# A recurrent attention with a gated MLP on one Trainium2 core: the attention's work written as a list of operations that the kernel sorts itself

## The chip, the cores and the metric

The kernel runs on one core of one Trainium2 chip. The time is the device's time for one launch in microseconds (us); three runs of the kernel before gave 843.01, 844.03 and 845.59, and their median, 844.03, is the number that the change is measured against. Five engines work side by side, each in its own fixed order of instructions: TensorE (PE in the profile; PEld is its loading of the stationary operand), VectorE (DVE), ScalarE (ACT), GpSimd (POOL) and SyncE (SP). They meet at semaphores. Here SP and POOL do little else than start transfers (DMA).

## The reference

A recurrence over 768 time steps for 4 x 8 heads of width 40, followed by an MLP over the 3072 tokens:

```python
state = np.zeros((B, H, D, D))                       # B, H, S, D = 4, 8, 768, 40
for t in range(S):
    y[:, :, t] = np.einsum('bhd,bhde->bhe', rt, state)
    Sa = np.einsum('bhde,bhe->bhd', state, at)
    state = state * wt[:, :, None, :] - np.einsum('bhd,bhe->bhde', Sa, bt)
    state = state + np.einsum('bhd,bhe->bhde', vt, kt)
x = y.transpose(0, 2, 1, 3).reshape(B * S, H * D)    # 3072 x 320
h = x @ w_in                                         # w_in 320 x 2048
g = h * np.tanh(np.log1p(np.exp(h)))
out = g @ w_out                                      # w_out 2048 x 320
```

The weights of the MLP come as 64-bit floats, everything else as 32-bit floats.

## The kernel before

**Attention in chunks.** The 768 steps are cut into 12 chunks of 64 (`C = 64`, `nch = 12`). Inside a chunk the recurrence becomes matrix products; only the state `ST` is carried from one chunk to the next. The 32 heads lie as two `be`, two `al` (on the partitions) and eight more, which a step takes in two halves `g`. The work has three parts:

- *Preparation*, `pre_a(c, be)`, 24 times. It loads the decays and `a` into `wa` and the rows of `b` and `k` into `bk` (L131 to L134, two buffers of each). On DVE it forms the running products of the decay, `P` forward (L147) and `E` backward (L157, written into `wa` over `a`, so that it stands behind the copies of `a` to `ad` by ACT, L155), and scales `a` (L152) and `bk` (L170). `P` goes to DRAM (L172, POOL's queue), for the MLP. PE multiplies `bk` by `ad` (L186); ACT and DVE take the results to `GP` and, masked, to `HA` (L188 to L193); PE transposes `bk` (L202), ACT copies it to `bkn`, and `bk` is free again.
- *Inverse*, `pre_inv(n)` and `post_inv(n)`, for two chunks at a time, six in all. DVE turns `GP` into `X` (`XL`, L209), does 30 pairs of a product (L214) and a sum (L216), in each of which every instruction needs the one before, and turns the result into `TT` (L218) and `T1` (L220). Then PE (L232, L241) and ACT make from it the blocks `bdT` (L249 to L251), and PE the operand `KT` of the recurrence from `HA` and `bdT` (L258, copied by ACT, L260).
- *Step*, `step(c)`, 12 times, each needing the step before. For each `g`: PE multiplies `KT` by `VS`, which holds the state and the values (L284), ACT takes it to `UVT` (L286), PE forms `pq` (L314) and transposes (L293, L304), DVE masks (L316), and PE sums output and new state (L334, L339); ACT copies the output to `yev` (L343), POOL's queue stores it (L370), and DVE updates the state (`stn` L342, `ST` L346).

**The MLP.** `M.run` takes 12 blocks of 256 tokens. `load_x` loads the attention's stored output and `P` and multiplies them (L565); `mlp1` (L583) is the first product with the weights split into a high and a low part, `mlp2` (L603 to L605) the second. Before it the weights are converted from 64 bits: a conversion loads a piece to `cv_d`, ACT writes a scaled copy to `cv_m` (L459), DVE puts the 32-bit number together in three instructions (L461 to L463) and ACT and DVE split it (L494, L495). `M.early` does the first quarter of `w_in`, `M.first` the other three, `M.second` three of the eight pieces of `w_out`, and `M.third`, within the MLP, the last five.

**What sets the order.** The order on each engine is made by the framework's scheduler, which takes instructions in the order of the program, as dependencies and free buffers allow, and moves parts of it ahead or back by an offset: `at(tc, k)` looks up the part's name in the table `OFF`, whose numbers are written by hand. `ORDER` says how steps, inverses and preparations follow each other in the program (the preparation of pair `n + 2` stands after the inverse of pair `n + 1`), `SORD` how the pieces of a step do. PSUM, eight banks, is cut into four pools of two: `ps_u` and `ps_q` for the steps, `ps_a` for the inverses, `ps_g` for the preparations; the MLP's matmuls use `ps_h` where `ps_a` and `ps_g` were.

Of the kernel before, what the change touches and what calls it, by code (L numbers as in the profile page):

```python
# [78 lines left out]
def attention(ctx, tc, I, yD, pD, nch, M):  # L79
# [35 lines left out]
    VS = [cs.tile([128, 2, 344], F32, name=f"VS{be}") for be in range(2)]
    UVT = cs.tile([128, 8, 256], F32, name="UVT")
    UVQ = [cs.tile([128, 16, 104], F32, name=f"UVQ{be}") for be in range(2)]
    bdr = [cs.tile([128, 2, 8, 2, 64], F32, name=f"bdr{i}") for i in range(NBR)] * (2 // NBR)
# [4 lines left out]
    RW, W2, HA, BKN, GP, KT = {}, {}, {}, {}, {}, {}
    LQ, SQ, OQ, PQ = (dict(S=SP, G=G, A=A)[x] for x in QS)

    def pre_a(c, be):
        n = 2 * c + be
        wa, bk, ad = wab[n % NWA], bkb[n % NWA], adb[n % 2]
        for al in range(2):
            q = slice(al * 64, al * 64 + 40)  # L130
            LQ.dma_start(out=wa[q], in_=I['wa'][c, be, al])  # L131
        for al in range(2):
            q = slice(al * 64, al * 64 + 40)
            LQ.dma_start(out=bk[q, :, 0:128], in_=I['bk'][c, be, al])  # L134
# [10 lines left out]
        V.tensor_reduce(out=w2[:, 0], in_=wz3[:, :, 1:33], axis=AX.X, op=ALU.mult)
# [512 lines left out]
```

## Time and profile before

| | before |
|---|---|
| runs | 843.01, 844.03, 845.59 us (median 844.03) |
| span of the profiled execution | 843.5 us |
| PE busy | 748.6 us (89%), 7816 instructions |
| DVE busy | 462.0 us (55%), 975 instructions |
| ACT busy | 429.0 us (51%), 937 instructions |
| POOL busy | 103.3 us (12%), 182 instructions |

The profile is of one execution, on its own clock from the span's start; its span is within the spread of the runs. In a row of instruction groups stand line, engine, operation, output and inputs with their shape, the count, then busy time and mean duration in ns, then the idle time of the engine just before them and what ended it. In a row of the timeline stand start, duration, engine, line, operation and shape, and in brackets how long it waited and for what. A weight load and its matmul are two records, and a row that joins several instructions gives their common stretch. L12 is line 12 of the kernel before, or, for lines of the changed kernel, of that one. Busy shares are means over stages with different limits, so a stage is read by itself.

### The profile page before, as it was taken

How to read it: one execution, taken by the hardware profiler on the slowest of the kernel's cores; microseconds unless marked ns; L12 is line 12 of the kernel's file. 1: busy time of each engine (PE TensorE's matmuls, PEld its weight loads, DVE VectorE, ACT ScalarE, POOL GpSimd, SP SyncE). 2: the span in 40 equal slices, each digit the busy share in tenths (PEclk: the TensorE clock that was granted, in tenths of full speed). 3: DMA queues.
4: the chain of work that ended last, by engine and by line, in shares of the span. 5: the costliest groups of instructions: out<-in, count | busy, mean ns of one | idle time of the engine just before them, and what ended most of it. 6: DMA issues, size and time to landing. Idle time of an engine off the chain costs nothing.

```text
span 843.5 us, 18796 instructions
## 1 busy us (share of the span) xinstructions
PE 748.6 (89%) x7816; PEld 695.6 (82%) x7816; DVE 462.0 (55%) x975; ACT 429.0 (51%) x937; POOL 103.3 (12%) x182
## 2 busy tenths in 40 slices
PE   2645898998989889889799899999999999999998
PEld 2534697887868778778768799999999999999998
DVE  6789879739899658788924639221222222122110
ACT  4533647774586866566738546333333333333331
POOL 8100012113122023221101200000000000000000
PEclk9855689899999999899959999999999999999999
DMA  6422223323423233323425734211120111100000
GB/s 177 134 71 64 74 63 73 90 67 105 129 81 80 66 88 103 82 67 96 123 66 142 179 109 128 54 35 36 38 54 25 31 54 35 35 21 16 16 1 32
DMA packets 58212, 61.91 MB, mean 73 GB/s; under 512 B 25536, under 2 KB 48704, under 8 KB 58128
## 3 DMA queue, kind: packets, MB, share of 16 engines
q1 hardware_dynamic: 49296, 40.94, 17.6%
q0 software_dynamic: 8832, 19.79, 9.5%
q8 instruction: 61, 1.00, 0.5%
q14 instruction: 23, 0.19, 0.1%
HBM read 48.79 MB, written 11.86 MB: 72 GB/s over the span
## 4 chain that ended last, share of the span: by engine, by line
PE 62%; DVE 15%; ACT 15%; issue 5%; DMA 2%; ACTq 0%; DVEq 0%; SPq 0%
PE ph L583 21%; PE po L604 7%; PE po L605 7%; PE po L603 7%; PE pa L186 5%; PE pa L258 4%; PE pq L314 3%; PE pq L334 2%; DVE XL L216 2%; DVE tmp L214 2%; ACT ad L155 2%; PE pu L284 1%; DMA cv_d<-in_wo 1%; DVE P L147 1%; ACT bdT L250 1%
## 5 line engine op out<-in xcount | busy, mean ns | idle before, releaser
L583 PE MATMUL ph<-xh,w_ih 128*128 128x256 f32 x576 | 148.3, 283 | 0.5 <-ACT xh L566 0.5
L585 ACT ACTIVATE g<-ph 128x512 f32<-128x512 f32 x96 | 57.3, 598 | 179.3 <-PE ph L583 179.2
L589 DVE TENSOR_TENSOR gl<-g,gh 128x1024 fp32r<-128x1024 f32 x48 | 58.7, 1225 | 160.7 <-ACT gh L588 160.4
L583 PE MATMUL ph<-xh,w_il 128*128 128x256 f32 x576 | 123.6, 283 | 0.0
L186 PE MATMUL pa<-bk,ad 128*128 128x168 f32 x384 | 85.0, 373 | 42.7 <-DVE bk L170 15.0
L604 PE MATMUL po<-w_ol,gh 128*128 128x320 f32 x384 | 118.8, 310 | 0.1
L605 PE MATMUL po<-w_oh,gl 128*128 128x320 f32 x384 | 118.4, 309 | 0.0
L603 PE MATMUL po<-w_oh,gh 128*128 128x320 f32 x384 | 117.7, 309 | 0.0
L186 PEld LDWEIGHTS pa<-bk,ad 128*128 128x128 f32 x384 | 70.8, 233 | 47.8 <-issue 22.8
L583 PEld LDWEIGHTS ph<-xh,w_ih 128*128 128x128 f32 x576 | 109.3, 190 | 0.7 <-ACT xh L566 0.7
L583 PE MATMUL ph<-xl,w_ih 128*128 128x256 f32 x384 | 101.2, 285 | 0.0
L583 PEld LDWEIGHTS ph<-xh,w_il 128*128 128x128 f32 x576 | 96.3, 190 | 0.0
L583 PEld LDWEIGHTS ph<-xl,w_ih 128*128 128x128 f32 x384 | 73.1, 190 | 0.8 <-issue 0.5
L604 PEld LDWEIGHTS po<-w_ol,gh 128*128 128x128 f32 x384 | 72.1, 188 | 0.5 <-DVE w_ol L495 0.5
L605 PEld LDWEIGHTS po<-w_oh,gl 128*128 128x128 f32 x384 | 72.1, 188 | 0.1
L603 PEld LDWEIGHTS po<-w_oh,gh 128*128 128x128 f32 x384 | 71.8, 188 | 0.0
L258 PE MATMUL pa<-bdT,HA 128*104 128x128 f32 x384 | 57.0, 304 | 9.0 <-ACT bdT L251 7.3
L258 PEld LDWEIGHTS pa<-bdT,HA 128*104 128x104 f32 x384 | 49.9, 190 | 14.4 <-ACT bdT L251 9.1
L216 DVE TENSOR_TENSOR XL<-XL,tmp 128x30 f32<-128x30 f32 (+9 forms) x180 | 59.0, 328 | 2.4
L214 DVE TENSOR_TENSOR tmp<-XL 128x30 f32<-128x30 f32 (+9 forms) x180 | 58.5, 325 | 2.5
L314 PE MATMUL pq<-bdr,UVT 128*128 128x128 f32 x384 | 57.3, 294 | 2.3 <-DVE UVQ L316 1.5
L314 PEld LDWEIGHTS pq<-bdr,UVT 128*128 128x128 f32 x384 | 50.8, 205 | 4.0 <-DVE UVQ L316 1.9
(89 smaller groups left out, 1243.5 us busy)
## 6 DMA issues: line engine op xcount, KB each, us to landing
wa<-in_wa SPq DMA_DIRECT2D x48, 162.5 KB
bk<-in_bk SPq DMA_DIRECT2D x48, 160.0 KB
cv_d<-in_wi SPq DMA_DIRECT2D x12, 512.0 KB
cv_d<-in_wo SPq DMA_DIRECT2D x8, 640.0 KB
pD<-P POOLq DMA_DIRECT2D x48, 81.2 KB, 2.2
VS<-in_vN POOLq DMA_DIRECT2D x24, 160.0 KB, 3.6
UVT<-in_vD POOLq DMA_DIRECT2D x24, 160.0 KB, 3.9
bdr<-in_rD POOLq DMA_DIRECT2D x24, 160.0 KB, 4.4
```

Of the source, the lines that this page charges most:

```text
L155: A.copy(ad[q, :, :, al], a[q].rearrange("p (s k t) -> p s k t", k=2, t=32))
L186: PE.matmul(pt[:, j], ad[:, s0 + j].rearrange("p k a t -> p (k a t)"), bk[:, s0 + j], start=(j == 0), stop=True, skip_group_check=True)
L214: V.tensor_tensor(out=tv, in0=X[:, i + 1:32, i:i + 1].broadcast_to([128, 31 - i, i]), in1=X[:, i:i + 1, 0:i].broadcast_to([128, 31 - i, i] ...
L216: V.tensor_tensor(out=X[:, i + 1:32, 0:i], in0=X[:, i + 1:32, 0:i], in1=tv, op=ALU.add)
L258: PE.matmul(pk[:, j], ha[:, s0 + j], bd[:, s0 + j].rearrange("p a t -> p (a t)"), start=(j == 0), stop=True, skip_group_check=True)
L314: PE.matmul(pq[:, s], UVT[:, g * 4 + s, be * 128:be * 128 + 128], br[:, be, g * 4 + s].rearrange("p a t -> p (a t)"), start=(s == 0), stop ...
L583: PE.matmul(o, w, x, start=(j == 0 and n == 0), stop=(n == 7), skip_group_check=True)
L585: A.activation(g[:, f0:f0 + 2], ph, AF.Mish)
L589: V.tensor_tensor(out=gl, in0=g, in1=gh.bitcast(F32), op=ALU.subtract)
L603: PE.matmul(po[k], gh[:, j, t], oh, start=(f == 0), stop=False, skip_group_check=True)
L604: PE.matmul(po[k], gh[:, j, t], ol, start=False, stop=False, skip_group_check=True)
L605: PE.matmul(po[k], gl[:, j, t], oh, start=False, stop=(f == 15), skip_group_check=True)
```

## The change

Every piece of the attention and of the early weight conversions becomes an operation of a list, `S.op(engine, cost, function, r=, w=)`: its engine, an assumed duration in us, what it reads and writes, and the function that issues its one instruction or its few of the same kind. From the reads and writes the list knows what each operation waits for. `Plan.order` then simulates the engines with the assumed durations: of the operations that can start within 0.05 us of the earliest it takes the one with the longest remaining path (`tail`), and puts the others off; the update of the state has 15 us added to its path (`LATE`). Sorted by the simulated starts, the operations are issued under `tc.manual_schedule()`, so that this order is the order on every engine, DMA issues included. The MLP's `run` is left to the scheduler as before, and is issued behind the list.

The instructions themselves stay, with these differences. PSUM is two pools of four banks, `psl` for the steps and `psr` for preparations and inverses, given out bank by bank. `E` has a tile of its own instead of lying in `wa`. `stn` has two buffers instead of one. A conversion scales `cv_d` in place, without `cv_m`; and the conversions are spread anew: the first quarter of `w_in` (`early`) as before from the start, quarters 1 and 2 (`first`, two buffers) once all preparations are issued, quarter 3 and three pieces of `w_out` (`second`, two buffers) once all preparations and inverses and the last step's operations stand. In the diff, cut to its core, the bodies of `pre_a`, `inv` and `step` are those of before with each call wrapped in `op`; two of them are shown.

```diff
-NA = 2
-NWA = 2
...
-OFF = {'I': 80, 'T1': 80, 'P00': -40, 'P10': 80, 'P11': 40, 'b0': 15, 'c0': 600, 'u0': -15, 'u1': 250, 'd0': 250,
...
-def at(tc, k):
-    return tc.high_priority(offset=OFF[k]) if OFF.get(k) else nullcontext()
+LATE = 15.0
...
+class Plan:
+    def __init__(self, look=0.05):
...
+    def order(self):
+        for o in reversed(self.ops):
+            o.tail = o.cost + o.lat + max((p.tail for p in o.post), default=0.0) + o.late
...
+            best = max((o for o in ready if o.eng == e and start[o] <= low[e] + self.look), key=lambda o: (o.tail, -o.i))
...
+        out.sort(key=lambda o: o.start)
+        return out
+    def issue(self):
+        bound = set()
+        for o in self.order():
+            for b in o.bufs:
+                if b not in bound:
+                    bound.add(b)
+                    b.t = b.pool[1][b.k]
+            o.fn()
...
-    ps_u = pool("ps_u", NU, space=PSUM)
-    ps_q = pool("ps_q", NQ, space=PSUM)
-    ps_a = pool("ps_a", NA, ictx, "right", space=PSUM)
+    ps_l = pool("ps_l", 1, space=PSUM)
+    ps_r = pool("ps_r", 1, ictx, "right", space=PSUM)
...
+    newL = S.pool("psl", 4, [ps_l.tile([128, 512], F32, name=f"pl{i}") for i in range(4)])
+    newR4 = S.pool("psr", 4, [ps_r.tile([128, 512], F32, name=f"pr{i}") for i in range(4)])
...
-        V.tensor_tensor_scan(out=E[:, 0:519][:, ::-1], data0=wz[:, 2:521][:, ::-1], data1=d1[:, 1:520][:, ::-1],
-                             initial=0.0, op0=ALU.mult, op1=ALU.add)
+        op('V', 1.15, lambda: V.tensor_tensor_scan(out=E[:, 0:519][:, ::-1], data0=wz[:, 2:521][:, ::-1], data1=d1[:, 1:520][:, ::-1],
+                                                   initial=0.0, op0=ALU.mult, op1=ALU.add), r=WZ + ['d1'], w=['E'])
...
+            op('V', 0.42, lambda: V.tensor_tensor(
+                out=st[:, :, 0:40].rearrange("p (s a) d -> p s a d", a=2), in0=stn.t.rearrange("p (s a) d -> p s a d", a=2),
+                in1=R.t.rearrange("p a s -> p s a").unsqueeze(3).broadcast_to([128, 4, 2, 40]), op=ALU.mult),
+               r=[(stn, 0), (stn, 2)] + [R], w=[('ST', g)], late=LATE)
...
+    M.early(S)
     for n in range(nds):
+        for c in (2 * n, 2 * n + 1):
+            for be in range(2):
+                pre_a(c, be)
+    preps = list(S.ops)
+    invs = []
+    for n in range(nds):
+        k = len(S.ops)
+        inv(n)
+        invs += S.ops[k:]
+        for c in (2 * n, 2 * n + 1):
+            step(c)
+    M.first(S, S.after(preps, lambda: (pctx.close(), M.open_first(S))))
+    M.second(S, S.after(preps + invs + S.ops[-1:], lambda: (ictx.close(), M.open_second(S))))
+    with tc.manual_schedule():
+        S.issue()
```

How the rows move is seen at three places. In such rows stand line, operation, output and inputs (a number behind a name tells buffers apart), shape, and how many alike follow each other. First DVE at the program's start, before: `wa_96` and `bk_98` belong to the first preparation, `cv_w` and `cv_d` to the first weight conversion.

```order
L461 TENSOR_SCALAR cv_w<-cv_m 128x512
L462 SCALAR_TENSOR_TENSOR cv_w<-cv_m,cv_w 128x512
L463 SCALAR_TENSOR_TENSOR cv_w<-cv_d,cv_w 128x512
L145 TENSOR_REDUCE w_138<-wa_96 128x8
L146 RECIPROCAL d_102<-w_138 128x8
L147 SCALAR_TENSOR_TENSOR P<-wa_96,d_102 128x520
L495 SCALAR_TENSOR_TENSOR w_il_928<-cv_w,w_ih_927 128x512
L150 COPY w_138<-P 128x8
L152 TENSOR_TENSOR wa_96<-wa_96,P 128x512
L156 RECIPROCAL d_102<-w_138 128x8
L157 SCALAR_TENSOR_TENSOR wa_96<-wa_96,d_102 128x519
L170 TENSOR_TENSOR bk_98<-bk_98,wa_96 128x8x128
```

And after, where the first preparation has `wa_88` and `bk_90`, the second `wa_89`:

```order
L264 TENSOR_REDUCE w_98<-wa_88 128x8
L264 TENSOR_REDUCE w_99<-wa_89 128x8
L265 RECIPROCAL d_94<-w_98 128x8
L266 SCALAR_TENSOR_TENSOR P_96<-wa_88,d_94 128x520
L268 COPY w_98<-P_96 128x8
L269 TENSOR_TENSOR wa_88<-wa_88,P_96 128x512
L270 RECIPROCAL d_94<-w_98 128x8
L271 SCALAR_TENSOR_TENSOR E<-wa_88,d_94 128x519
L265 RECIPROCAL d_94<-w_99 128x8
L277 TENSOR_TENSOR bk_90<-bk_90,E 128x8x128
```

The conversion's four instructions stood ahead of and among the first preparation's; now the first two preparations follow each other, and `E` is written to its own tile.

Second DVE in the middle of an inverse, before, the first one (L214 and L216 are its chain; L146 to L170 are preparations of later chunks):

```order
L214 TENSOR_TENSOR tmp<-XL 128x238
L146 RECIPROCAL d_102<-w_868 128x8
L216 TENSOR_TENSOR XL<-XL,tmp 128x17x14
L147 SCALAR_TENSOR_TENSOR P<-wa_97,d_102 128x520
L214 TENSOR_TENSOR tmp<-XL 128x240
L150 COPY w_868<-P 128x8
L152 TENSOR_TENSOR wa_97<-wa_97,P 128x512
L216 TENSOR_TENSOR XL<-XL,tmp 128x16x15
L170 TENSOR_TENSOR bk_98<-bk_98,wa_96 128x8x128
L214 TENSOR_TENSOR tmp<-XL 128x240
L156 RECIPROCAL d_102<-w_868 128x8
L216 TENSOR_TENSOR XL<-XL,tmp 128x15x16
```

And after, the second one (L343 and L346 are the chain, L472 the masks of a step):

```order
L346 TENSOR_TENSOR XL<-XL,tmp 128x20x11
L343 TENSOR_TENSOR tmp<-XL 128x228
L346 TENSOR_TENSOR XL<-XL,tmp 128x19x12
L343 TENSOR_TENSOR tmp<-XL 128x234
L346 TENSOR_TENSOR XL<-XL,tmp 128x18x13
L472 TENSOR_TENSOR UVQ_116<-pl_160,cst 128x8x64
L472 TENSOR_TENSOR UVQ_117<-pl_161,cst 128x8x64
L472 TENSOR_TENSOR UVQ_116<-pl_158,cst 128x8x64
L472 TENSOR_TENSOR UVQ_117<-pl_159,cst 128x8x64
L343 TENSOR_TENSOR tmp<-XL 128x238
L346 TENSOR_TENSOR XL<-XL,tmp 128x17x14
L343 TENSOR_TENSOR tmp<-XL 128x240
```

The chain's links stood among other chunks' preparation; now they follow each other, and in the middle stand the four masks of one step together.

Third PE behind an inverse of the middle of the attention, before (the fifth), with `TT` and `X` of the inverse (L232, L241, L258), a preparation's products and transposes (L186, L202), and a step (L284, from `KT` and `VS`):

```order
L232 MATMUL pa<-TT,GP 32x32
L186 MATMUL pa<-bk_99,ad_101 128x168 x6
L232 MATMUL pa<-TT,GP 32x32 x12
L186 MATMUL pa<-bk_99,ad_101 128x168 x2
L232 MATMUL pa<-TT,GP 32x32 x19
L202 MATMUL pa<-cst,bk_99 128x128 x8
L241 MATMUL pa<-X_4209,GP 32x32 x32
L258 MATMUL pa<-bdT_103,HA 104x128 x8
L284 MATMUL pu<-KT,VS_116 64x64 x8
L258 MATMUL pa<-bdT_104,HA 104x128 x8
L284 MATMUL pu<-KT,VS_117 64x64 x8
```

And after, behind the fourth inverse and the last products (L502) of the step that follows it; L306 and L329 are the preparation's products and transposes, L457 transposes the state:

```order
L502 MATMUL pl_159<-bdr,smd_142 64x2x64 x4
L306 MATMUL pr_165<-bk_90,ad_92 128x168 x2
L329 MATMUL pr_163<-cst,bk_90 128x128 x4
L329 MATMUL pr_164<-cst,bk_90 128x128 x4
L306 MATMUL pr_162<-bk_91,ad_93 128x168 x3
L457 MATMUL pl_160<-cst,ST_119 128x128 x4
L457 MATMUL pl_161<-cst,ST_120 128x128 x4
L306 MATMUL pr_165<-bk_91,ad_93 128x168 x3
L306 MATMUL pr_162<-bk_91,ad_93 128x168 x2
L329 MATMUL pr_163<-cst,bk_91 128x128 x4
L329 MATMUL pr_164<-cst,bk_91 128x128 x4
```

Preparation stood in between the inverse's and the step's matmuls; now the last of its products and its transposes, which free `bk_90` and then `bk_91`, stand behind the whole step.

More of the change, by code (lines that the diff above doesn't have):

```diff
@@ L110, in attention @@
         G.memset(b, 0.0)
-    for t in [d1] + [x.rearrange("p s k a t -> p (s k a t)") for x in adb[:NAD]]:
+    for t in [d1] + [x.rearrange("p s k a t -> p (s k a t)") for x in adb]:
         A.copy(t, z.broadcast_to(t.shape))
-    for t in bdT:
-        G.memset(t, 0.0)
[L115 to L118, printed above, removed]
@@ L119, in attention @@
-    ST = [cs.tile([128, 8, 64], F32, name=f"ST{g}") for g in range(2)]
-    for t in VS + [UVT] + bdr[:NBR] + ST:
-        G.memset(t, 0.0)
+    VS = tiles(cs, 2, [128, 2, 344], "VS")
+    UVT = cs.tile([128, 8, 256], F32, name="UVT")
+    UVQ = tiles(cs, 2, [128, 16, 104], "UVQ")
+    bdr = cs.tile([128, 2, 8, 2, 64], F32, name="bdr")
+    ST = tiles(cs, 2, [128, 8, 64], "ST")
+    newBKN = make(wk, NBKN, [128, 664], "bkn")
+    newKT = make(wk, NKT, [104, 8, 128], "KT")
+    newRW = make(wk, 4, [128, 2, 16], "rw")
@@ L300, in step_d, with tr @@
             return None
-        smd = wk.tile([128, 4, 128], F32, name="smd", bufs=2)
-        pt = ps_u.tile([128, 4, 128], F32, name="pu")
-        for s in range(4):
-            PE.transpose(pt[:, s], st[:, 2 * s:2 * s + 2].rearrange("p a d -> p (a d)"), ident)
-        A.copy(smd, pt)
+        smd, b = newSMD(), newL()
+        dv = lambda: view(b, full, 512, "p (s x) -> p s x", s=4)
+        def tr():
+            for s in range(4):
+                PE.transpose(dv()[:, s], st[:, 2 * s:2 * s + 2].rearrange("p a d -> p (a d)"), ident)
@@ new lines, in w_in, with w_out, cv @@
+    def w_in(self, wp, q):
+        self.ih.append(wp.tile([128, 3, 512], F32R, name=f"w_ih{q}"))
+        self.il.append(wp.tile([128, 3, 512], F32R, name=f"w_il{q}"))
+    def w_out(self, wp, q):
+        self.oh.append(wp.tile([128, 640], F32R, name=f"w_oh{q}"))
+        self.ol.append(wp.tile([128, 640], F32R, name=f"w_ol{q}"))
+    def cv(self, n, w, ctx=None):
+        p = self.tc.tile_pool(name=n, bufs=1, side="right")
+        p = ctx.enter_context(p) if ctx else self.cvx.enter_context(p)
+        return p.tile([128, w], F32, name="cv_w"), p.tile([128, w, 2], I32, name="cv_d")
@@ L533, in second, with first, open_second @@
+    def first(self, S, key):
+        new = S.pool("cva", 2)
+        ops = [self.plan_in(S, new, q, k, [key]) for q in (1, 2) for k in range(3)]
+        S.after(ops, lambda: self.cvx.close())
+    def open_second(self, S):
         self.ps_h = self.pool("ps_h", NH, space=PSUM)
-        if NQ1 < 4:
-            wp = self.wp = self.pool("w2b", 1)
-            with self.tc.tile_pool(name="cvb", bufs=CVB, side="right") as cv:
-                self.w_in(wp, cv, range(NQ1, 4))
         self.mpx = self.pool("mpx", 2)
@@ L539, in second @@
         self.mpa = self.pool("mpa", 2)
[L540 to L543 removed]
+        wp = self.pool("w2d", 1)
+        self.w_in(wp, 3)
+        for q in range(NO1):
+            self.w_out(wp, q)
+        self.cvx = ExitStack()
+        S.cvd[:] = [self.cv(f"cvd{i}", 640) for i in range(2)]
+    def second(self, S, key):
+        new = S.pool("cvd", 2)
+        ops = [self.plan_in(S, new, 3, k, [key]) for k in range(3)]
+        ops += [self.plan(S, new, lambda q=q: (self.oh[q], self.ol[q]), self.I['wo'][:, q * 640:(q + 1) * 640], [key], ('wo', q))
+               for q in range(NO1)]
+        S.after(ops, lambda: self.cvx.close())
```

607 lines of the change are left out of this document (348 added, 259 removed).

## The prediction

> **What bounds the kernel now.** After the page I cut the span into four stages by what ends each: the first inverse (99.2 us), the sixth and last inverse (418.2), the attention's last matmuls (494), the end. Columns: stretch, its length, then busy time (and instructions) of PE, PEld, DVE, ACT and POOL, granted TensorE clock, DMA share, GB/s.
>
> ```profile
> 0.00:99.20 99.20, 50.48 (x222) 42.35 (x222) 80.16 (x182) 44.58 (x121) 24.62 (x46) 0.74 0.38 106
> 99.20:418.20 319.00, 281.61 (x4062) 249.95 (x4062) 254.91 (x638) 214.18 (x545) 67.87 (x120) 0.95 0.34 88
> 418.20:494.00 75.80, 70.74 (x877) 58.56 (x878) 35.09 (x60) 41.61 (x85) 9.86 (x14) 0.86 0.46 115
> 494.00:843.50 349.50, 345.75 (x2663) 344.78 (x2659) 91.87 (x97) 128.68 (x187) 1.00 (x2) 1.00 0.15 42
> ```
>
> The last stage, the MLP, is TensorE without a gap, and the change does not touch it. The first is DVE (80 of 99 us) with PE half idle: no recurrence step can run before the first inverse. In the second no engine is full by itself: DVE 80%, PE 88%. Where the inverses stand, where the MLP ends and how fast it runs:
>
> ```profile
> L209 DVE STREAM_TRANSPOSE XL<-GP x6: 2090/2124/2155, 49.9 to 375.2; 128x1024 f32<-128x1024 f32 x6
> L218 DVE STREAM_TRANSPOSE TT<-XL x6: 1931/1976/2023, 97.2 to 416.2; 128x1024 f32<-128x1024 f32 x6
> L605 PE MATMUL po<-w_oh,gl x384: 307/308/414, 504.5 to 839.6; 128*128 128x320 f32 x192
> 550.00:750.00 200.00, 200.00 (x1525) 200.00 (x1525) 47.61 (x48) 70.92 (x102) 0.00 (x0) 1.00 0.14 38
> ```
>
> The first inverse begins at 49.9 (L209) and its result stands at 97.2 + 2.0 = 99.2: 49 us for one inverse. Six ends in 418.2 - 99.2 = 319 us make a period of 63.8 us for two chunks. The MLP has 48 calls of `mlp1` with 32 matmuls and 48 of `mlp2` with 24, 2688 in all; at 200 / 1525 = 0.131 us each it needs 352.5 us, and from the last matmul's end (839.9) to the span's end are 3.6 us. So my sum has four terms: first inverse T0, five periods P, the tail from the last inverse to the first MLP matmul, and 352.5 + 3.6.
>
> **Part 1, the first inverse.** Two groups hold the inverse's chain, and its links wait for each other:
>
> ```profile
> L216 DVE TENSOR_TENSOR XL<-XL,tmp 128x30 f32<-128x30 f32 (+9 forms) x180 | 59.0, 328 | 2.4
> L214 DVE TENSOR_TENSOR tmp<-XL 128x30 f32<-128x30 f32 (+9 forms) x180 | 58.5, 325 | 2.5
> ```
> ```profile
> 410.12 0.32 DVE L216 TENSOR_TENSOR XL<-XL,tmp 128x150 f32<-128x150 f32 x1
> 410.48 0.29 DVE L214 TENSOR_TENSOR tmp<-XL 128x130 f32<-128x130 f32 x1
> ```
>
> One inverse is (59.0 + 58.5) / 6 = 19.6 us of 60 links, 0.04 between links (410.12 + 0.32 to 410.48), say 2.1, and the transposes 2.1 and 2.0: 25.8 us when nothing stands between. The first one took 49, for the scheduler put other chunks' preparation between its links; in the new order two short masks stand there. Ahead of it are four preparations. They began late, with a conversion in front:
>
> ```profile
> 5.91 0.47 DVE L461 TENSOR_SCALAR cv_w<-cv_m 128x512 int32<-128x512 int32 x1 [2.84 <-ACT cv_m L459]
> ...
> 7.75 0.41 DVE L145 TENSOR_REDUCE w<-wa 128x8 f32<-128x256 f32 x1
> ```
> ```profile
> DVE wa L157 <- ACT ad L155: 11.0, 10, 2.9
> ```
>
> From 7.75 to 49.9 are 42.1 us. Out of it go three conversions of 7.75 - 5.91 and an L495 (512 wide, 0.7), 2.5 each, now behind the inverse, and three waits of L157 for ACT, 1.1 each (11.0 / 10), since `E` has a tile of its own: 31.3. They start at 5.9 instead of 7.75, so the inverse at 37.2. PE is as cold there as before (clock 0.74); for loads of `bk` that wait on it I allow 2. T0 = 39.2 + 25.8 = 65, against 99.2.
>
> **Part 2, the period.** Between two inverses the new order is a chain across engines. PE does post-inverse and one whole step first; only then the last preparation matmuls (L306) and the transposes (L329) that free a `bk` buffer; then the buffer is reloaded and multiplied (L277) on DVE, where the rest of two preparations and the inverse are queued behind. PE's and ACT's links at full clock:
>
> ```profile
> 372.59 0.84 PE L186 MATMUL pa<-bk,ad 128*128 128x168 f32 x4 [0.34 <-DVE HA L191]
> ...
> 382.72 1.99 PE L258 MATMUL pa<-bdT,HA 128*104 128x128 f32 x16
> ...
> 386.52 2.05 PE L314 MATMUL pq<-bdr,UVT 128*128 128x128 f32 x16 [0.33 <-ACT UVT L286]
> 388.41 1.04 PE L293 MATMUL pu<-cst,UVT 128*128 128x128 f32 x8
> ...
> 390.15 1.15 PE L284 MATMUL pu<-KT,VS 104*64 104x64 f32 x32
> ...
> 396.74 0.88 PE L334 MATMUL pq<-UVQ,bkn 128*64 128x104 f32 x16
> 397.45 0.61 PE L339 MATMUL pq<-bdr,smd 128*64 128x128 f32 x8
> ```
> ```profile
> 369.59 0.41 ACT L249 COPY bdT<-TT 32x256 f32<-32x256 f32 x1 [0.29 <-DVE TT L218]
> ...
> 377.83 1.49 ACT L251 COPY bdT<-pa 32x256 f32<-32x256 f32 x4
> ...
> 406.30 1.07 ACT L260 COPY KT<-pa 104x512 f32<-104x512 f32 x2
> ```
>
> (A matmul is two records, a transpose one; about 0.2 us at a row's end is overlapped by the next.) From TT's end: ACT makes eight bdT copies of 0.41, an X copy (512 wide, 0.54) and two short evictions (as one L249), to 4.2, then L251's four, to 5.7. PE's L393 waits for them: two rows like L258's, with PSUM handed back tile by tile, 4, to 9.7; hand-off 0.3 and the last KT copy, to 10.6. The step: L429's second row (as L284) to 11.8, with 0.3 and the UVT copy to 12.6; L469 (two rows like L314's, 3.5) starts on the first group at 12.1 and ends at 15.6; L442 (two like L293's, 1.8) to 17.4; four times L497 and L502 (0.72 + 0.44) to 22. Two L306 and eight L329 (as L293) make 1.5: the first `bk` buffer is free at 23.6. The second follows at 28, and its load is in before DVE comes to it. The reload, in a stretch with little else on the queues:
>
> ```profile
> 351.87 1.63 SPq L134 DMA_DIRECT2D bk<-in_bk  x2
> ```
> ```profile
> 355.00:356.00 1.00, 1.00 (x15) 0.88 (x16) 0.49 (x2) 0.00 (x0) 0.00 (x0) 0.79 0.39 113
> 356.00:357.00 1.00, 1.00 (x20) 0.93 (x16) 0.97 (x3) 0.42 (x1) 0.68 (x2) 1.00 0.00 0
> ```
>
> Issued at 351.9, nothing moves after 356: 4.1 to 4.3 us, so L277 starts at 27.9. DVE's prices:
>
> ```profile
> L316 DVE TENSOR_TENSOR UVQ<-pq,cst 128x512 f32<-128x512 f32 x48 | 32.9, 688 | 24.4 <-PE pq L314 24.3
> L147 DVE TENSOR_TENSOR_SCAN P<-wa,d 128x520 f32<-128x520 f32 x24 | 29.6, 1233 | 0.3
> L170 DVE TENSOR_TENSOR bk<-bk,wa 128x1024 f32<-128x1024 f32 x24 | 29.1, 1214 | 0.1
> L191 DVE TENSOR_TENSOR HA<-pa,cst 128x192 f32<-128x192 f32 (+1 forms) x72 | 23.7, 330 | 25.7 <-ACT HA L190 23.5 <-PE pa L186 2.0
> L346 DVE TENSOR_TENSOR ST<-stn,R 128x320 f32<-128x320 f32 x22 | 10.6, 484 | 0.1
> ```
>
> Independent instructions overlap by 0.08. From the first L277 to the inverse stand, in the new DVE order, two L277 (1.14 each), four scans (1.15), two L269 (as L316, 0.61), nine masks (L314 and L317, 0.27) and eight small ones (half a mask, an estimate): 2.3 + 4.6 + 1.2 + 2.4 + 1.1 = 11.6, with 0.4 for a mask that waits for its evictions 12. The inverse now carries the other step's DVE work and two masks between its links: four L472 (0.61), four L507 (as masks, 0.25), two L513 (0.4), 0.5, less 0.4 of hidden gaps: 25.8 + 4.3 = 30.1. P = 27.9 + 12 + 30.1 = 70. That other step's PE work (L393, then 11.4 us as above) runs under the inverse from 36 and ends, with the masks' wait, near 61; POOL's stores of P stand behind the step's yD, and are back before L277.
>
> Then the clock: PE rests some 9 us at the end of each inverse (61 to 70) and starts the chain cold:
>
> ```profile
> 352.18 3.58 PE L314 MATMUL pq<-bdr,UVT 128*128 128x128 f32 x16
> ```
> ```profile
> 348.00:355.00 7.00, 6.87 (x42) 5.73 (x41) 4.00 (x10) 2.19 (x5) 0.00 (x0) 0.54 0.11 32
> ```
>
> For 7 us the clock was half, and sixteen L314 took 3.58 instead of 2.05. One such spell at the start of a period costs between nothing (ACT's copies bind there) and 3.4; I take 2: P = 72, bounds 67 and 76. The Trainium skill, "TensorE: Matmul & The Clock Gate", section "HAM oscillation", has the rule that speaks against an order that lets PE rest: an idle window of about 3.4 us halves the clock, a busy one restores it. By that rule the spell lasts one window and P would be about 71.7 (an estimate); the trace agrees on the two levels, with a longer spell here.
>
> The last period has no later preparation on DVE, 2 less. T5, the last inverse's end, is 65 + 4 x 72 + 70 = 423, against 418.2: the start's 34 us are given back over five periods, which were 63.8 before since eight preparations ran ahead of the first.
>
> **Part 3, the tail.** What the new order has done by then is one step more and fewer conversions:
>
> ```profile
> 0.00:418.20 418.20, 8.69 (x18) 0.90 0.35 92
> ```
>
> (L346 alone: 18 of 22, so nine steps; three were left.) Now two are left, for one step stands behind each inverse and one inside it. Step 10 ends on PE 22 - 1.8 + 2 = 22 after the last inverse (no L306 between, the cold start), step 11 from the same links (VS copies 0.9, L429 2.2, UVT 0.9, L469 3.5, mask 1, L497 and L502 4.6) 13 later, 35. But of twelve conversions that DVE now does after the last inverse, ten stand ahead of the first MLP load's product, 17 of their instructions behind step 11's masks (at 33). At 0.47 (above) to 0.8, 0.65 each: 11, with ACT's turns 13, to 46. The product to the first MLP matmul took
>
> ```profile
> 465.67 0.96 DVE L565 TENSOR_TENSOR xy<-xy,xp 128x768 f32<-128x768 f32 x1 [0.66 <-DMA xp<-pD]
> ```
> ```profile
> 467.58 0.74 PE L583 MATMUL ph<-xh,w_ih 128*128 128x256 f32 x4 [0.47 <-ACT xh L566]
> ```
>
> 1.9, so the tail is 48 (bounds 37, PE alone, and 58). The last `w_in` quarter is converted under the first three; for its being late, 3.
>
> **The sum.** 423 + 48 + 3 + 352.5 + 3.6 = 830.1 against a span of 843.5. The runs' median, 844.0, is 0.5 above that span: 830.6.
>
> **Rivals.** (a) *Slower, by a cold PE.* From L393 to the free buffer PE's own links are 3.5 + 2.2 + 3.5 + 1.8 + 4.6 + 1.5 = 17.1 us at full clock. If the clock stays down through half of them more, each costs 0.75 more (3.58 / 2.05): 6.4 a period, 862. It decides from a mean P of 74.3 (65 + 5 x 74.3 + 407 = 843.5), 2.7 above mine: less than 4 us of such work. For it: the mean clock of 0.74 where PE was half idle; against it: 0.95 in the second stage, and the links stand close together. 21%. (b) *DVE hardly waits.* If PE and the reload come earlier than I add them, P falls to DVE's own work, 70 less the 9 that it now waits: 61, and the time to 776. For it: DVE's prices are the surest in the sum; against it: L277 waits for that buffer whatever else DVE does. 10%. (c) *The weights are late*,
>
> ```profile
> ACT cv_m L459 <- DMA cv_d<-in_wo: 5.1, 3, 2.8
> ```
>
> whose loads made ACT wait 1.7 in three cases. With 1.7 for each of the ten, the tail grows by 17: 848. For it: all loads are now behind the preparations; against it: two buffers instead of one. 7%. (d) *No change*: P of 74 gives the start's gain back exactly; 9%.
>
> **Numbers.** Forecast 53%, its own range 812 to 841 (P 68.5 to 74). The range 806 to 857 leaves out (b) and half of (a). Faster by over 0.3% (2.5 us, about what a measurement of this kernel can tell from no change): forecast and (b), 0.63; within, 0.09; slower, (a) and (c), 0.28.
>
> **What would show it.** TT's first end near 65, then ends 70 to 73 apart, the last near 423; DVE idle some 4 us ahead of an L277 and 5 more on the step's masks in each period; PE's clock at half under each inverse's end; the first MLP matmul near 471, none ahead of the attention's last. Wrong: a first TT beyond 75, periods under 66 or over 76, PE idle within the MLP.

## The result and the profile after

The changed kernel takes 892.44 us (median of four runs, 891.75 to 897.87) where the kernel before took 844.81 beside it: 5.85 per cent more, ratio 1.0585 with a 95% interval of 1.053 to 1.064. Run again later (e9), it took 894.64 beside 844.27, ratio 1.0605 (1.054 to 1.067). The profiled execution was the longest of the four, 897.87 us; that of e9 has a span of 890.7, so that differences of spans between runs are good to some 5 us. The forecast was faster: 830.6, in a range of 806 to 857. The kernel is slower instead, and the time lies above that range.

The stages of the profiled execution (span 895.7 us), cut at each inverse's end and at the first MLP matmul; columns as in the prediction.

```profile
0.00:72.40 72.40, 27.32 (x120) 23.50 (x120) 54.84 (x126) 24.47 (x66) 21.07 (x40) 0.70 0.39 97
72.40:154.56 82.16, 61.26 (x832) 57.36 (x832) 60.30 (x145) 46.82 (x122) 15.08 (x24) 0.81 0.30 80
154.56:237.09 82.53, 63.20 (x864) 58.88 (x864) 61.20 (x145) 47.50 (x123) 15.10 (x24) 0.83 0.31 80
237.09:318.15 81.06, 61.48 (x864) 56.63 (x864) 57.67 (x137) 45.64 (x120) 15.09 (x24) 0.86 0.28 75
318.15:400.05 81.90, 61.81 (x864) 57.15 (x864) 57.64 (x137) 45.72 (x120) 15.11 (x24) 0.85 0.28 74
400.05:481.26 81.21, 62.71 (x856) 58.46 (x856) 52.66 (x124) 44.26 (x117) 13.06 (x20) 0.84 0.23 63
481.26:536.66 55.40, 39.73 (x728) 38.12 (x728) 32.83 (x58) 35.99 (x75) 6.99 (x10) 0.78 0.51 158
536.66:895.70 359.04, 355.67 (x2688) 355.17 (x2688) 100.64 (x113) 135.13 (x195) 0.00 (x0) 0.99 0.16 44
```

The first inverse ends 26.8 us earlier than before (99.2 to 72.4). Then each period takes 81 to 82.5 us, almost alike, in which PE and DVE both rest for some 20 us: two engines with about 60 us of work each need 82, so for a good part of a period one of them works while the other waits. Over the five periods that is 408.9 us instead of 319, so the last inverse ends at 481.3, which is 63.1 later than the 418.2 of before. From there to the first MLP matmul pass 55.4 us instead of 49.4. The MLP's own stage is 16.9 shorter (359.0 against 843.5 - 467.6), since it no longer carries the attention's last steps. 63.1 + 6.0 - 16.9 is 52.2, the difference of the spans.

How a period passes: PE in the third one, TT standing at 237.09 (the timeline, rows that matter).

```profile
237.14 3.62 PE L361 MATMUL pr<-TT,GP 32*32 32x32 f32 x128 [8.14 <-DVE TT L348]
240.69 2.05 PE L306 MATMUL pr<-bk,ad 128*128 128x168 f32 x6
242.67 1.92 PE L369 MATMUL pr<-X,GP 32*32 32x32 f32 x64
244.52 2.05 PE L306 MATMUL pr<-bk,ad 128*128 128x168 f32 x6
246.36 4.42 PE L393 MATMUL pr<-bdT,HA 128*104 128x128 f32 x32
250.71 2.08 PE L429 MATMUL pl<-KT,VS 104*64 104x64 f32 x64
...
262.82 0.61 PE L502 MATMUL pl<-bdr,smd 128*64 128x128 f32 x8
263.36 0.84 PE L306 MATMUL pr<-bk,ad 128*128 128x168 f32 x4
264.03 1.04 PE L329 MATMUL pr<-cst,bk 128*128 128x128 f32 x8
```

Its continuation on SP's queue (the reload of the buffer that L329 freed) and on DVE:

```profile
265.33 1.60 SPq L249 DMA_DIRECT2D bk<-in_bk  x2
```
```profile
272.75 1.23 DVE L277 TENSOR_TENSOR bk<-bk,E 128x1024 f32<-128x1024 f32 x1 [5.44 <-DMA bk<-in_bk]
...
281.27 1.23 DVE L277 TENSOR_TENSOR bk<-bk,E 128x1024 f32<-128x1024 f32 x1 [1.55 <-DMA bk<-in_bk]
...
287.79 2.15 DVE L338 STREAM_TRANSPOSE XL<-GP 128x1024 f32<-128x1024 f32 x1
```

This is the closed chain of the prediction, link by link: inverse, PE's whole step, release of `bk`, reload, the rest of the preparation on DVE, inverse. Little of one link overlaps the next. An inverse takes DVE 26 to 32 us here, and from its end to the next one's start pass 50 to 52 (237.1 to 287.8 in this period). In the kernel before, with preparation between their links, the inverses took 37 to 50 us, and 3 to 43 passed between them, 18 on average.

### The profile page after: what moved, and what is told of

Its sections match the earlier page's. It is cut to its first block, busy times and chain, and to the rows that moved or that the text cites. A ratio compares the mean times of both kernels' runs of the same rounds, so it can differ in the third digit from the quotient of the medians.

```text
span 895.7 us, 18823 instructions
## 1 busy us (share of the span) xinstructions
PE 733.2 (82%) x7816; PEld 705.3 (79%) x7816; DVE 477.8 (53%) x975; ACT 425.5 (48%) x937; POOL 101.5 (11%) x166
## 4 chain that ended last, share of the span: by engine, by line
PE 66%; DVE 17%; DMA 6%; ACT 6%; issue 3%; POOL 1%; SPq 1%; DVEq 0%; ACTq 0%; POOLq 0%
PE ph L751 21%; PE pr L306 7%; PE po L772 6%; PE po L773 6%; PE po L771 6%; DVE XL L346 5%; DVE tmp L343 5%; DMA bk<-in_bk 4%; PE pl L469 3%; PE pr L393 3%; PE pl L497 3%; PE pl L442 3%; PE pr L361 2%; PE pr L369 2%; DMA wa<-in_wa 2%
## 5 line engine op out<-in xcount | busy, mean ns | idle before, releaser
L306 PE MATMUL pr<-bk,ad 128*128 128x168 f32 x384 | 97.3, 418 | 52.9 <-ACT HA L313 17.8
L306 PEld LDWEIGHTS pr<-bk,ad 128*128 128x128 f32 x384 | 82.2, 266 | 60.5 <-ACT HA L313 20.2
L751 PEld LDWEIGHTS ph<-xl,w_ih 128*128 128x128 f32 x384 | 73.8, 192 | 0.1
L361 PE MATMUL pr<-TT,GP 32*32 32x32 f32 x768 | 21.7, 236 | 61.7 <-DVE TT L348 53.2
L771 PEld LDWEIGHTS po<-w_oh,gh 128*128 128x128 f32 x384 | 72.2, 188 | 0.0
L773 PEld LDWEIGHTS po<-w_oh,gl 128*128 128x128 f32 x384 | 72.1, 188 | 0.0
L772 PEld LDWEIGHTS po<-w_ol,gh 128*128 128x128 f32 x384 | 72.1, 188 | 0.0
L361 PEld LDWEIGHTS pr<-TT,GP 32*32 32x32 f32 x768 | 21.0, 151 | 63.0 <-DVE TT L348 34.8
L346 DVE TENSOR_TENSOR XL<-XL,tmp 128x30 f32<-128x30 f32 (+9 forms) x180 | 59.6, 331 | 5.6
L343 DVE TENSOR_TENSOR tmp<-XL 128x30 f32<-128x30 f32 (+9 forms) x180 | 59.6, 331 | 5.5
L393 PE MATMUL pr<-bdT,HA 128*104 128x128 f32 x384 | 54.8, 309 | 2.7 <-ACT HA L313 1.0
L393 PEld LDWEIGHTS pr<-bdT,HA 128*104 128x104 f32 x384 | 52.8, 201 | 4.6 <-ACT KT L396 1.6
```

What stands on the lines that cost most here:

```text
L306: PE.matmul(pv()[:, j], ad[:, s0 + j].rearrange("p k a t -> p (k a t)"), bk[:, s0 + j], start=(j == 0), stop=True, skip_group_check=True)
L343: op('V', 0.16 + m * i * 0.001, lambda tv=tv, i=i, m=m: V.tensor_tensor(out=tv, in0=X[:, i + 1:32, i:i + 1].broadcast_to([128, m, i]), in1 ...
L346: op('V', 0.16 + m * i * 0.001, lambda tv=tv, i=i: V.tensor_tensor(out=X[:, i + 1:32, 0:i], in0=X[:, i + 1:32, 0:i], in1=tv, op=ALU.add), ...
L361: PE.matmul(xv()[al * 32:al * 32 + 32, j], gp.t[q, u, 0], TT[q, u], start=(j == 0), stop=True, skip_group_check=True)
L393: PE.matmul(kv()[:, j], ha.t[:, s0 + j], bd[:, o + s0 + j].rearrange("p a t -> p (a t)"), start=(j == 0), stop=True, skip_group_check=True)
L751: PE.matmul(o, w, x, start=(j == 0 and n == 0), stop=(n == 7), skip_group_check=True)
```

## The experiments

Theory A: the order makes a period one closed chain, because the whole step stands on PE between an inverse and the release of `bk`. Theory B: the half clock after PE's rest is what makes it long. Theory C: any fixed order costs this, since it can't react. The comparison of each run is with the kernel before, beside it on the chip. In the last column e5, e7, e10 and e12 have their first MLP matmuls ahead of the last step's last ones; the others follow from 518.1 in e5, 452.6 in e7, 551.9 in e10 and 491.4 in e12.

| run | us | before | ratio (95%) | inverses end | first MLP matmul |
|---|---|---|---|---|---|
| changed kernel | 892.44 | 844.81 | 1.0585 (1.053 to 1.064) | 72.4 to 481.3 | 536.7 |
| e1 LATE 10 | 851.03 | 839.87 | 1.0113 (1.006 to 1.017) | 73.8 to 432.0 | 487.9 |
| e2 no reload of bk | 874.35 | 839.87 | 1.0402 (1.034 to 1.046) | 68.1 to 460.8 | 514.5 |
| e3 no step loads | 892.48 | 839.87 | 1.0616 (1.056 to 1.068) | 72.3 to 475.0 | 530.4 |
| e4 PE kept busy, 32 | 890.40 | 839.87 | 1.0587 (1.052 to 1.066) | 72.2 to 474.9 | 529.3 |
| e5 conversions early | 882.05 | 842.95 | 1.0453 (1.039 to 1.052) | 72.1 to 478.8 | 510.3 |
| e6 third bk buffer | 874.26 | 842.95 | 1.0377 (1.031 to 1.045) | 74.6 to 457.6 | 512.9 |
| e7 other numbers | 812.73 | 842.95 | 0.9638 (0.957 to 0.971) | 83.1 to 407.3 | 443.6 |
| e8 other numbers, third buffer | 825.49 | 842.95 | 0.9789 (0.973 to 0.985) | 76.6 to 407.6 | 462.9 |
| e10 scheduler | 908.54 | 844.27 | 1.0772 (1.071 to 1.084) | 87.0 to 506.0 | 540.8 |
| e11 PE kept busy, 38 | 879.02 | 844.27 | 1.0418 (1.036 to 1.048) | 71.5 to 463.9 | 517.5 |
| e12 e7 with loads of 2.5 us | 851.72 | 844.27 | 1.0103 (1.007 to 1.014) | 76.6 to 443.6 | 479.8 |

**e1.** One number of the list:

```diff
-LATE = 15.0
+LATE = 10.0
```

> One number of the list, LATE, is 10 instead of 15: the same operations, but the transposes that free the bk buffers (L329) stand ahead of the step's matmuls on PE and not behind them. Theory A (a period is one closed chain, in which the whole step stands between an inverse and the reload of bk): the step's 12 to 15 us leave the chain, periods of 68 to 72 us instead of 82, 830 to 850 us in all. Theory B (PE's half clock after its rest makes the period long, whatever the order): the rest under the inverse stays, periods of 79 or more, 880 us or more. Theory C (any fixed order costs this, since it can't react to what the chip does): 870 to 895 us.

The period falls from 81.8 to (432.0 - 73.8) / 5 = 71.6 us, as theory A has it; the time, 851.03, is 1 us above A's range and far below those of B and C. The same instructions, sorted with one other number, are 4.5 per cent faster (1.0113 against 1.0585). The clock still falls in this kernel (0.53 from 226 to 237, behind an inverse), so B does not carry the 52 us. The one number moves other operations too, so e1 shows what the order is worth, and not the place of these transposes alone. Where the `bk` transposes now stand, PE's order behind the fourth inverse (L393 makes the step's KT):

```
L361 MATMUL pr_165<-TT,GP_153 32x32 x32
L369 MATMUL pr_165<-X_156,GP_153 32x32 x32
L306 MATMUL pr_165<-bk_91,ad_93 128x168 x3
L306 MATMUL pr_163<-bk_91,ad_93 128x168 x3
L306 MATMUL pr_162<-bk_91,ad_93 128x168 x2
L329 MATMUL pr_164<-cst,bk_91 128x128 x4
L329 MATMUL pr_165<-cst,bk_91 128x128 x4
L393 MATMUL pr_163<-bdT_102,HA_148 104x128 x4
```

The buffer is free before the step begins, and not behind it.

**e2.** The loads of `bk` only for the first chunk (L277's multiply is a minimum for the later ones):

```diff
-            op('S', 0.1, lambda q=q, al=al: SP.dma_start(out=bk[q, :, xo:xo + 128], in_=I['bk'][c, be, al]), w=[('bk', be, al)], lat=2.5)
+            op('S', 0.1, lambda q=q, al=al: SP.dma_start(out=bk[q, :, xo:xo + 128], in_=I['bk'][c, be, al]) if c == 0 else None, w=[('bk', be, al)], lat=2.5)
```

> bk is loaded for the first chunk only, later preparations work on what is in the buffers (their loads of bk and the use of that data are left out; the multiply of L277 becomes a minimum for them); the order on every engine is that of the changed kernel. Theory A: L277 follows PE's release of the buffer instead of a landing 7.4 us later, for the first of the two buffers in full and for the second in part: 7 to 9 us less in each of five periods, 848 to 860 us. Theory B: the clock is as before, a gain of at most the 5 us per period that DVE waited: 867 us or more.

15 to 18 us faster (by the ratios and by the medians), half of what I expected of A: 874.35 lies above A's range, and in the one that I had given to B. DVE in its third period, TT standing at 225.0:

```profile
256.17 1.22 DVE L277 TENSOR_TENSOR bk<-bk,E 128x1024 f32<-128x1024 f32 x1
259.83 0.42 DVE L264 TENSOR_REDUCE w<-wa 128x8 f32<-128x256 f32 x1 [2.44 <-DMA wa<-in_wa]
...
271.87 2.16 DVE L338 STREAM_TRANSPOSE XL<-GP 128x1024 f32<-128x1024 f32 x1
```

The L277 comes 31.2 us after TT instead of 35.7. Then DVE waits 2.44 for the next load, that of `wa`, where the changed kernel does not wait at this place; when the inverse begins, 3.8 of the 4.5 us are left (271.87 - 225.0 = 46.9 after TT instead of 50.7). The reload is a link, and not the largest.

**e3.** The step's loads left out after the first chunk, those of UVT and in the same way those of VS and bdr:

```diff
-            op('G', 0.75, lambda q=q, al=al: G.dma_start(out=UVT[q, :, 64:192], in_=I['vD'][c, al]), w=[('UVv', al, 0), ('UVv', al, 1)], lat=2.5)
+            op('G', 0.75, lambda q=q, al=al: G.dma_start(out=UVT[q, :, 64:192], in_=I['vD'][c, al]) if c == 0 else None, w=[('UVv', al, 0), ('UVv', al, 1)], lat=2.5)
```

> The loads of the step's VS, UVT and bdr are left out after the first chunk (the later chunks work on its data); the order is otherwise that of the changed kernel. Theory A with contention (the reload of bk takes 7.4 us instead of the 4.2 of my sum because the step's loads are issued in the same microseconds): landing 4.5 to 5.5 us after issue, 2 to 3 us less per period, 875 to 883 us. If the reload takes 7.4 us by itself: no change, 889 to 895 us.

No change in the time. The reload lands little earlier:

```profile
261.77 1.63 SPq L249 DMA_DIRECT2D bk<-in_bk  x2
```
```profile
268.04 1.23 DVE L277 TENSOR_TENSOR bk<-bk,E 128x1024 f32<-128x1024 f32 x1 [4.29 <-DMA bk<-in_bk]
```

268.04 - 261.77 is 6.3 us where the changed kernel has 7.4. The step's loads are worth 1 us of it, so contention with them falls as the main reason. Contention as such does not. The two loads of `bk` are 0.33 MB. In the changed kernel the DMA engines moved 1.33 MB from the issue to the L277 (178 GB/s for 7.45 us), here still 0.99 MB (158 GB/s for 6.27 us), for the stores of the step's output and the loads of `wa` go on beside them. In the quiet stretch of the prediction they moved 0.33 MB in 4.13 us, these loads alone. No run leaves the stores and `wa` out, so that their traffic is the reason is likely and not shown.

**e4 and e11.** Matmuls of the identity ahead of the first L361 of each inverse but the first, 32 in e4 and 38 in e11:

```diff
             def mx(h=h, xv=xv, b=bx):
+                for _ in range(32 if h == 0 and n else 0):
+                    PE.matmul(b.t[:, 0:128], ident, ident, start=True, stop=True, skip_group_check=True)
```

> 32 matmuls of the identity with itself (7.7 us at full clock) are put ahead of the first L361 of each inverse but the first, into the PSUM bank that L361 then overwrites: PE does not rest in the last 8.5 us of an inverse. Theory A: the granted clock under the inverse's end goes from 0.5 to near 1, but behind it ACT's copies bind, so 3 to 4 us less per period, 870 to 880 us. Theory B: the half clock is what makes the period long: 7 to 10 us less per period, 842 to 860 us.

> As e4, with 38 matmuls of the identity instead of 32 (8.7 us for a rest of 8.5), since in e4 a rest of 1.4 us was left and the clock fell again behind three of five inverses. Theory A: the clock holds behind all inverses, 3.4 us less per period as where it held in e4 (77.7 instead of 81.1), 872 to 880 us where the changed kernel has 889 to 892. Theory B: 850 us or less.

In e4 a rest of 1.0 to 1.4 us was left, and its time lies in neither theory's range. That rest made a difference. PE behind two inverses of e4, and the clock behind them (stretches as before, the clock is the third number from the right):

```profile
237.50 2.21 PE L363 MATMUL pr<-TT,GP 32*32 32x32 f32 x128 [1.02 <-DVE TT L348]
...
315.19 2.69 PE L363 MATMUL pr<-TT,GP 32*32 32x32 f32 x128 [1.43 <-DVE TT L348]
```
```profile
237.00:242.00 5.00, 4.50 (x199) 4.21 (x199) 5.00 (x6) 4.30 (x11) 0.00 (x0) 1.00 0.08 14
...
315.00:320.00 5.00, 4.81 (x142) 4.39 (x144) 5.00 (x8) 3.89 (x10) 0.00 (x0) 0.66 0.08 16
320.00:325.00 5.00, 5.00 (x77) 4.81 (x74) 3.75 (x10) 3.12 (x10) 1.02 (x2) 0.50 0.26 87
```

Behind the rest of 1.02 us the clock held, and that period took 77.7 us; behind the four of 1.43 to 1.44 it fell, and e4's mean period was 80.5, where e9 has 80.7. In e11, without a rest, it is 1.00 in the same places. There the first period, behind the inverse that has no such matmuls ahead of it, still takes 82.2; the four others take 77.5 on average, where e9 has 80.8 and the first profile 81.7. So a cold start costs a period 3.3 to 4.2 us. The time is 15.6 us below e9's beside it, as A had it (872 to 880). The clock is worth these 15.6 us, and the roughly 35 us that remain of the loss are not its doing: B falls as the whole reason and stands as a part.

**e5.** The six conversions of `first` ahead:

```diff
         ops = [self.plan_in(S, new, q, k, [key]) for q in (1, 2) for k in range(3)]
+        for o in ops:
+            o.late = 100.0
```

> The six conversions of first (quarters 1 and 2 of w_in) have 100 us added to their path in the list, so that they are taken as soon as they can start; nothing else is changed. Theory A for the tail (PE's 14.7 us of rest ahead of the MLP are the first load of x, which waits for the last of these six conversions): PE's rest ahead of the first MLP matmul falls to 1 to 5 us, 8 to 13 us less in all, 879 to 884 us. Rival: the conversions that come after them are late in their place, or the inverses wait for them: 888 to 896 us.

10.4 us faster by the medians, as expected. In the changed kernel PE rested 14.72 ahead of the MLP, and the load of x left SP's queue when the last of these conversions was done:

```profile
521.46 0.69 DVE L652 SCALAR_TENSOR_TENSOR w_il<-cv_w,w_ih 128x512 fp32r<-128x512 f32 x1 [0.70 <-ACT w_ih L651]
```
```profile
522.18 0.33 SPq L606 DMA_DIRECT2D xy<-yD  x1
```
```profile
536.66 1.23 PE L751 MATMUL ph<-xh,w_ih 128*128 128x256 f32 x4 [14.72 <-ACT xh L734]
```

In e5 that load is issued at 454.0. Two MLP matmuls stand at 510.3, ahead of the last step's, and the others follow from 518.10, right behind the attention's last (517.56 + 0.61). From the last inverse to there are 39.3 us, where the changed kernel has 55.4 (54.1 in e9).

**e6.** A third `bk` buffer, and the buffers taken in turn:

```diff
-    bkb = tiles(cp, 2, [128, 8, 168], "bk")
+    bkb = tiles(cp, 3, [128, 8, 168], "bk")
...
-        wa, bk, ad = wab[be], bkb[be], adb[be]
+        bi = (2 * c + be) % 3
+        wa, bk, ad = wab[be], bkb[bi], adb[be]
```

> A third bk buffer, taken in turn; costs and LATE as in the changed kernel, the list sorts itself anew. Theory A in the form that the buffer closes the chain: a preparation no longer waits for the release of a buffer by the matmuls behind the step, DVE's 7 us of waiting for bk per period go, periods of 72 to 76 us, 855 to 868 us. Theory A in the form that the step's place on PE closes it, whatever the buffers (the last products of a preparation stay behind the step): periods of 79 or more, 880 us or more.

874 us and periods of 76.6, between the two forms. The wait of DVE for `bk` shrinks from 31.9 to 23.4 us in total and does not go: the last products of a preparation still stand behind the step. DVE's masks of `HA` wait 25.4 us for these products, where the changed kernel has 8.3.

**e7, e8 and e12.** Other numbers of the list; e7's (the 5.1 stands for the other loads and for yD's store as well, and goes back to 2.5 in e12):

```diff
-LATE = 15.0
+LATE = 4.8
...
-    def __init__(self, look=0.05):
+    def __init__(self, look=0.08):
...
-            op('S', 0.1, lambda q=q, al=al: SP.dma_start(out=wa[q], in_=I['wa'][c, be, al]), w=[('wz', be, al), ('a', be, al)], lat=2.5)
+            op('S', 0.1, lambda q=q, al=al: SP.dma_start(out=wa[q], in_=I['wa'][c, be, al]), w=[('wz', be, al), ('a', be, al)], lat=5.1)
...
-            op('P', 0.29 * m, mm, r=[('ad', be, 0), ('ad', be, 1), ('id', be)] + BK, w=[b], mode=128, claim=[gp, ha])
+            op('P', 0.29 * m, mm, r=[('ad', be, 0), ('ad', be, 1), ('id', be)] + BK, w=[b], mode=128, claim=[gp, ha], late=2.0)
...
         ops = [self.plan_in(S, new, q, k, [key]) for q in (1, 2) for k in range(3)]
+        for o in ops:
+            o.late = 100.0
```

> The list with other numbers: LATE 4.8 instead of 15, a load assumed to take 5.1 us instead of 2.5, 2 us added to the path of the preparation's products (L306) and 100 to that of first's conversions, and a choice among operations that start within 0.08 us. Two bk buffers as before. Theory A: preparation no longer stands behind steps, and the load of x is not late: periods of 62 to 68 us, the last inverse near 400, 815 to 830 us. Theory C (a fixed order as such is dearer than the scheduler's): not below 840 us.

> The list with other numbers and a third bk buffer: LATE 11.3, a load assumed to take 3.9 us, 9.6 us added to the path of the transposes (L329), 2 to that of L306 and 10 to that of first's conversions, a choice within 0.02 us. Theory A: as e7, with the last inverse near 395, 813 to 828 us. Theory C: not below 840 us.

> As e7, but a load is again assumed to take 2.5 us. If the list's wrong duration for loads is a large part of the loss (loads land 4 to 7 us after their issue): preparation again waits for loads in its place and the order loses most of what e7 won, 850 to 885 us. If LATE and the two added paths make e7's order: 813 to 825 us.

e7 beats both kernels: 812.73 us, 3.6 per cent below the kernel before and 9 below the changed one, with the same instructions in a fixed order; that is 2 us below its range of 815 to 830. e8 is within its range. Both are well below the 840 of C, so a fixed order is not dear as such. DVE's rest ahead of the instructions that first use the loads of `bk` and `wa` (the groups of instructions; the last column), first in the changed kernel, then in e7, then in e12:

```profile
L277 DVE TENSOR_TENSOR bk<-bk,E 128x1024 f32<-128x1024 f32 x24 | 29.0, 1208 | 31.9 <-DMA bk<-in_bk 31.9
...
L264 DVE TENSOR_REDUCE w<-wa 128x8 f32<-128x256 f32 x24 | 9.7, 404 | 16.8 <-DMA wa<-in_wa 16.8
```
```profile
L277 DVE TENSOR_TENSOR bk<-bk,E 128x1024 f32<-128x1024 f32 x24 | 29.2, 1218 | 4.1 <-DMA bk<-in_bk 3.6
...
L264 DVE TENSOR_REDUCE w<-wa 128x8 f32<-128x256 f32 x24 | 9.6, 405 | 7.5 <-DMA wa<-in_wa 7.5
```
```profile
L277 DVE TENSOR_TENSOR bk<-bk,E 128x1024 f32<-128x1024 f32 x24 | 29.3, 1219 | 27.2 <-DMA bk<-in_bk 17.2 <-PE pl L429 5.1 <-PE pr L306 4.9
...
L264 DVE TENSOR_REDUCE w<-wa 128x8 f32<-128x256 f32 x24 | 9.8, 416 | 26.2 <-DMA wa<-in_wa 18.8 <-PE pr L289 7.4
```

That is 48.7 us in the changed kernel, 11.6 in e7 and 53.4 in e12, where only the assumed duration of a load went back to 2.5 us, and 39 us of e7's gain went with it. These waits alone do not make the time: e12 has more of them than the changed kernel and is 41 us faster. And e12 loses in one place. Its second period takes 113.2 us where e7's takes 73.1; its four others together take 253.9, e7's 251.1. In that period the third inverse takes DVE 75 us (182.0 to 257.3), with whole preparations between its links.

Such preparations stand between the links of e7's inverses too, as in the kernel before: from the second on an inverse takes 47 to 53 us there, and from its end to the next one's start pass 1 to 26. In the changed kernel these were 26 to 32 and 50 to 52. e7's first inverse ends later than the changed kernel's (83.1), and its periods of (407.3 - 83.1) / 5 = 64.8 us are those of the kernel before (63.8). PE goes to the first MLP matmuls, which stand inside the attention's last step, without a gap:

```profile
442.72 1.09 PE L457 MATMUL pl<-cst,ST 128*128 128x128 f32 x8
443.57 0.36 PE L753 MATMUL ph<-xh,w_ih 128*128 128x256 f32 x1
```

**e9** is the changed kernel again (above); its mean period is 80.7 us where the first profile has 81.8. **e10** issues the sorted list without `tc.manual_schedule()`:

> The changed kernel once more, beside the three that follow, as the measure for them: 5.3 to 6.4 per cent over the kernel before, as at its first run.

> The list is sorted and issued as in the changed kernel, but without the manual schedule: the framework's scheduler takes the operations in the list's order and moves them as it does in the kernel before. Theory A (it is this order that is bad, above all the step ahead of the last preparation): the scheduler brings preparation forward in part, periods of 70 to 78 us, 845 to 880 us. Theory C (a fixed order as such is the loss): within 1 per cent of the kernel before.

e10 is slower still, 908.54 us, with periods of 83.8, outside both expectations: C falls, and with it my expectation of A that the scheduler would mend the order. It starts from the list's order, puts conversions ahead of the first preparation again, and ends the first inverse at 87.0.

## Why the prediction was wrong, step by step

The sum had four terms against the span. Measured, they were: T0 72.4 instead of 65 (+7.4), five periods 408.9 instead of 358 (+50.9), the tail 55.4 instead of 48 (+7.4), and the MLP with its late weights 359.0 instead of 352.5 + 3.6 + 3 = 359.1. Together 65.6, the distance from 830.1 to 895.7. The step that failed is the period P of part 2, taken as 72 and measured as 81.8: its 50.9 us alone turn a gain of 13 us into a loss. The mechanism was right, a closed chain across the engines; the links that were off were all taken too short. P was already longer there than the 63.8 of before; what the sum counted on was the early first inverse, and a chain of the true length eats that up and more.

- *Part 2, "L277 starts at 27.9", with 2 more for the clock: 35.7.* Of these 5.8 us, 3.4 are the reload. I took 4.1 to 4.3 us from one quiet stretch; here it took 7.4 (265.33 to 272.75), 0.3 more from the buffer's release to the issue, and 6.3 with the step's loads gone (e3). The other 2.4 are PE: between L361 and L393 stand six L306, two rows of 2.05 us at half clock, that my list of PE's links did not have, though its rest (9.7 us to L393's end, where the trace has 250.7 - 237.1 = 13.6) allowed for ACT. The clock was half for some 11 us (rows below) and cost 3.3 to 4.2 us per period by e11, where I took 2.
- *"With 0.4 for a mask that waits, 12" for the second part: 15.0.* The second L277 waits 1.55 for its reload, which I had as in by then: on SP's queue a load of `wa` stood ahead of it and waited for DVE (rows below). And masks wait for L306 on a PE that has cooled again (clock 0.50 from 276 to 280). The inverse itself, 30.1, was 30.4.
- *Part 1.* The inverse's 25.8 us were right (72.4 - 46.1 = 26.3). Its start at 39.2 was 46.1: where I took out conversions and waits for `ad`, DVE waited for loads of `wa` and `bk` instead, 1.46 + 2.57 + 2.38 + 2.27 us. Which wait would come next I had not asked there.
- *Part 3.* The tail came out of the DVE order, 46 us to the first product of x. It is the load of that x which was late (e5): it waits for `first`'s last conversion, then 12.6 us to L733.
- *The bounds.* P lay in 67 to 76 by bounds for each link that knew only the clock, and none for a load beside other traffic. Rival (a) named the side and the point (a mean P over 74.3), by the clock alone; e11 gives the clock 15.6 us. The signs at the prediction's end were the right ones: a period over 76 was named as what would show it wrong.

Who waited for whom on SP's queue from 266 to 277 us in the changed kernel (in total, times, longest), the issue that then followed, and the clock behind the third inverse:

```profile
SPq L246 <- DVE E L271: 6.9, 1, 6.9
```
```profile
275.89 1.59 SPq L249 DMA_DIRECT2D bk<-in_bk  x2
```

```profile
240.00:244.00 4.00, 4.00 (x86) 3.58 (x82) 3.43 (x8) 2.29 (x7) 0.49 (x1) 0.50 0.27 87
244.00:248.00 4.00, 4.00 (x38) 3.81 (x34) 2.39 (x5) 2.64 (x8) 0.54 (x2) 0.53 0.16 42
248.00:252.00 4.00, 4.00 (x70) 3.85 (x70) 2.70 (x7) 3.62 (x8) 1.01 (x2) 1.00 0.05 12
```

What stays open: how the loss, and e7's gain, are shared among the order's places. The orders differ in many places, only waits, periods and the inverses' stretches were compared, and no run moves preparation into the inverses by itself. That x's tile lies where the buffers of these conversions were is read from the code; e5 shows the dependence, not its kind.

## What to carry to other kernels

On a closed chain across engines little hides a link, so an error in a link's size adds up nearly in full and times the number of rounds: list every instruction that the new order puts on the chain, and take a load's time from a stretch with the traffic that it will have beside it, with a bound above it. Work taken out from between the links of a serial stretch must go somewhere: here it came to stand on the chain. An order that a list sorts is only as good as its assumed numbers: here one priority was worth 40 us and one assumed load duration 39 (nearly all in one of five periods), and a wrong one costs more than the hand-set order that it replaces. When such an order is slow, change its numbers before judging fixed orders as such.

## What the hardware showed that I had not expected

Behind each of four rests of PE of 1.43 to 1.44 us, at the end of an inverse and with 32x32 matmuls behind them, the granted clock fell to 0.50 (e4); behind the one rest of 1.02 us it stayed at 1.00. After a rest of 8.1 us the clock stayed at half for some 11 us from PE's start at 237.1, with PE without a gap (0.50 and 0.53 to 248, 1.00 from there). The Trainium skill, "TensorE: Matmul & The Clock Gate", section "HAM oscillation", gives idle gaps of over about 3.4 us as what takes the clock down; these traces show a shorter rest that suffices, before small matmuls.

Two loads of 40 partitions each, issued on SP in 1.6 us, were in use 7.4 us after the first issue, with 1.33 MB moved in that time, and still 6.3 with the step's loads gone and 0.99 MB moved; 0.33 MB of it are these loads.
